# PSUM tiles for down projections, and the order and split of ready weights, in a fused attention, MoE and SwiGLU kernel

## The chip, the cores and the metric

One core of one Trainium2 chip runs the kernel. The metric is the device time of that core for one execution, in microseconds; lower is better. Before the change it is 2129.76 us, the median of three runs.

## The reference

Three stages run one after the other (setup and parameter names left out):

```python
def _attn_ref(q, k, v):
    # B, H, S, D = 4, 8, 576, 64; heads 0-3 see the last 32 positions, heads 4-7 every 32nd
    scores = scale * np.matmul(q, k.transpose(0, 1, 3, 2))
    scores = np.where(masks[None], scores, -1000000000.0)
    attn = np.exp(scores - np.max(scores, axis=-1, keepdims=True))
    return np.matmul(attn / (np.sum(attn, axis=-1, keepdims=True) + 1e-09), v)

def _moe_ref(x, w_gate, w1, w2):
    # N, D, E, F = 2304, 512, 8, 1024
    logits = x @ w_gate
    P = np.exp(logits - logits.max())
    for _ in range(8):
        P /= P.sum(1, keepdims=True) + 1e-09
        P /= P.sum(0, keepdims=True) + 1e-09
        P *= N / E
    for e in range(E):
        out += P[:, e:e + 1] * (np.maximum(x @ w1[e], 0.0) @ w2[e])
    return out

def _moe2_ref(x, w_gate, w_val, w_out, rms_g):
    # 2304 tokens, d_model 512, d_ff 1536
    xn = x / np.sqrt(np.mean(x * x, axis=-1, keepdims=True) + 1e-06) * rms_g
    g = xn @ w_gate
    return g * (1.0 / (1.0 + np.exp(-g))) * (xn @ w_val) @ w_out
```

## The kernel before

Every large matrix product is made of high and low halves in the 32-bit format fp32r, three matmuls for each product (high by high, high by low, low by high). A product of two-by-two blocks is done with seven block products in place of eight, so sums and differences of blocks ("combos") are prepared for tokens and weights, and results are added up again in several places.

The program has four stretches. Until about 320 us it runs attention and expert 0. From there to about 1600 us it runs experts 1 to 7 in 42 groups: `n` counts groups, a group is an expert `g`, a half `hh` of its width and a third `qd` of the tokens. A group has two rounds of seven up products. Each is six matmuls of 128x384 columns (L1215) into one of two PSUM tiles of a bank, `ub0` and `ub1`, which VectorE (L1247) and ScalarE (L1358, L1362) empty. After each up product stands one down unit (L1817): nine matmuls of 128x256 columns, which belong to the group 12 slots earlier. Two units make a down product `k` (0 to 6), which fills three times 256 columns of PSUM. Then `evict_1` adds these to `acc`, by ScalarE (L1838) for products 0, 2, 3 and 4 of most groups, by VectorE (L1849) for the rest, or, in the last expert, in three pieces by VectorE (L1843).

From about 1600 to 1725 us lies the transition: the last group's downs, the RMS norm, transposes of the normed tokens on TensorE (L1465, emptied at L1466 by VectorE), the splitting of them (L1482, L1483), their stores to `xnd` in HBM (L1492, L1516) and the loads of token blocks (L1147). From there to the end there are nine passes over the SwiGLU layer (a third of its width by a third of the tokens). Their up products are again L1215 (finished at L1383, L1401, L1404, L1418), and each of their downs is three matmuls of 128x512 columns (L729 to L731) into one of six PSUM banks. `evict` empties a bank by ScalarE in the first third (L2110) and by VectorE after that (L2112).

PSUM has eight banks. Two hold `ub`. The other six are a pool with three tiles, made in `begin_psum`, which follows readers and writers by the tile:

```python
pool = ctx.enter_context(tc.tile_pool(name="db", bufs=1, space=PSUM, reuse_waits="tile"))
three, two, one = (pool.tile([P, 512 * n], F32, name=f"db{n}") for n in (3, 2, 1))
threes = [three[:, :768], two[:, :768], three[:, 768:]]
```

`PAIR` gives a down product its place: products 0 and 2 write the first 768 columns of `three` (A), products 1, 3 and 5 those of `two` (B), products 4 and 6 the last 768 of `three` (C). The transposes use `one`. In the first two groups the column sums of the routing matrix (Sinkhorn) are a matmul with ones (`columns_1`, L715) into a free part of the `ub` tile just emptied; VectorE reads it at L719.

The weights of the SwiGLU layer are prepared during the experts. `first_combos` makes the combos of the first quarter's weights in high and low and stores them to `w1d` in HBM (L924), with the seven products in the order `SPOTS`; `ready_combos` loads them back during the transition (L938), one product or two at a time. Second weights lie as plain numbers in `m2o`; `prepare_2` loads one tile to a single buffer in `fa` (L1080), ScalarE writes the high half to `w2t` (L1083) and VectorE the low half (L1086).

Who runs when: each engine runs its instructions in program order. Program order comes from helper queues. `Background.pump` is called once per slot; a `Queue` gives out a step when its lag (in slots: `STEP` 1.5, `PACE` 1.2, `WRITE` 3, `READ` 7) is over, in turn; `follow` is an `add` that starts from now; `later` calls a function some slots later, outside the queues; `drain` brings a tagged step forward at the latest point of its use. Nearly all loads and stores of these stretches are issued on SyncE's queue, the `y1d` traffic on GpSimd's.

## Time and profile before

| what | value |
|---|---|
| runs | 2129.76 us median of 3 (2123.81 to 2134.14) |
| profiled execution, its own time | 2127.49 us |
| its span in the trace | 2124.7 us |
| mean granted TensorE clock | 0.985 |
| TensorE matmuls busy | 2027.7 us (95%) |
| weight loads busy (beside matmuls) | 1926.7 us (91%) |
| VectorE busy | 1594.4 us (75%) |
| ScalarE busy | 1312.5 us (62%) |
| GpSimd busy | 268.4 us (13%) |
| moved by DMA | 434.24 MB, mean 204 GB/s |

Busy shares are means over the four stretches, and TensorE's busy time contains modelled ends of matmuls, so that a short wait may not show as idle time. A weight load (PEld) stands ahead of each matmul; where it waits, the matmul behind it waits less, by what was still running. Times in the trace are counted from the span's start.

### The profile page before, as it was taken

Reading aid. Unit: us, or ns where it says so; the run is one execution under the profiler, and the core shown is the slowest. Engines: PE = TensorE matmul, PEld = TensorE weight load, DVE = VectorE, ACT = ScalarE, POOL = GpSimd, SP = SyncE. Lnnn points to the kernel's source line nnn. Section 1 sums busy time; section 2 is a strip of 40 time slices with the busy share of each in tenths; the row PEclk is TensorE's granted clock in tenths of the full one; section 3 lists DMA queues with packets and bytes.
Section 4 is the critical chain, followed back from the end, with each engine's and each line's share of the span. In section 5 each row is a group of like instructions: output and inputs, shape, how many; then the busy total and the mean of one; then the engine's idle time right before and its main releaser. Section 6 shows DMA issues by size and latency. Waiting matters only on the chain. (4 is left out here: it accounts for less than half of the span.)

```text
span 2124.7 us, 37479 instructions
## 1 busy us (share of the span) xinstructions
PE 2027.7 (95%) x13611; PEld 1926.7 (91%) x13611; DVE 1594.4 (75%) x3387; ACT 1312.5 (62%) x2932; POOL 268.4 (13%) x304
## 2 busy tenths in 40 slices
PE   8999998999999999999999999999997689999998
PEld 7888888999999999999999999999997578888897
DVE  4677656878787887868778787887987567877644
ACT  6766334777776877778777777777755333423422
POOL 6444200001111111111111111111100000000000
PEclk9999999999999999999999999999998899999999
DMA  7687675577978979798887978869657764443331
GB/s 188 165 247 197 197 250 181 210 247 178 279 210 216 264 204 296 202 245 224 237 250 193 264 185 239 225 165 281 185 158 261 232 202 155 131 174 115 129 134 60
DMA packets 358249, 434.24 MB, mean 204 GB/s; under 512 B 80944, under 2 KB 260336, under 8 KB 358064
## 3 DMA queue, kind: packets, MB, share of 16 engines
q1 hardware_dynamic: 319296, 363.48, 52.2%
q0 software_dynamic: 38768, 68.36, 18.6%
q8 instruction: 107, 1.75, 0.3%
q14 instruction: 78, 0.64, 0.1%
HBM read 301.75 MB, written 130.02 MB: 203 GB/s over the span
## 5 line engine op out<-in xcount | busy, mean ns | idle before, releaser
L1215 PE MATMUL ub<-xt,w1t 128*128 128x384 f32 x2328 | 475.4, 341 | 29.2 <-DVE fa L1404 14.2
L1215 PEld LDWEIGHTS ub<-xt,w1t 128*128 128x128 f32 x2328 | 401.5, 192 | 36.5 <-DVE fa L1404 14.8
L1215 PE MATMUL ub<-xx,w1t 128*128 128x384 f32 x1956 | 396.4, 339 | 10.5 <-DVE fa L1247 3.8
L1817 PE MATMUL db<-w2t,ht 128*128 128x256 f32 x2772 | 383.0, 283 | 6.5 <-DVE acc L1849 3.3
L1817 PEld LDWEIGHTS db<-w2t,ht 128*128 128x128 f32 x2772 | 368.2, 190 | 11.1 <-DVE acc L1849 7.1
L1817 PE MATMUL db<-w2t,hx 128*128 128x256 f32 x2520 | 349.6, 284 | 7.2 <-DVE acc L1849 3.8
L1215 PEld LDWEIGHTS ub<-xx,w1t 128*128 128x128 f32 x1956 | 333.8, 190 | 18.4 <-DVE fa L1247 6.9
L1817 PEld LDWEIGHTS db<-w2t,hx 128*128 128x128 f32 x2520 | 333.2, 190 | 16.2 <-DVE acc L1849 12.5
L1247 DVE TENSOR_TENSOR fa<-ub,fa 128x384 f32<-128x384 f32 x360 | 199.2, 554 | 149.2 <-PE ub L1215 134.9
L1366 ACT ACTIVATE fa<-fa 128x384 f32<-128x384 f32 x252 | 132.3, 525 | 180.6 <-DVE fa L1247 180.3
L1881 POOL DMA_DIRECT2D y1d<-acc x99 | 113.9, 1150 | 843.6 <-ACT acc L1874 378.3
L1243 DVE TENSOR_TENSOR ht<-fa,ht 128x384 fp32r<-128x384 f32 x344 | 189.4, 552 | 33.0 <-ACT ht L1240 32.3
L1240 ACT ACTIVATE ht<-fa 128x384 fp32r<-128x384 f32 x344 | 177.4, 518 | 37.9 <-DVE fa L1418 37.4
L1874 ACT ACTIVATE acc<-acc,prob 128x256 f32<-128x256 f32 (+1 forms) x351 | 190.8, 573 | 14.3 <-DVE acc L1849 14.0
L1243 DVE TENSOR_TENSOR hx<-fa,hx 128x384 fp32r<-128x384 f32 x316 | 174.4, 552 | 27.9 <-ACT hx L1240 26.6
L1240 ACT ACTIVATE hx<-fa 128x384 fp32r<-128x384 f32 x316 | 162.1, 519 | 48.7 <-DVE fa L1418 47.4
L1321 DVE TENSOR_TENSOR fa<-fa 128x384 f32<-128x384 f32 x336 | 185.6, 552 | 5.3 <-ACT fa L1362 0.3
L1358 ACT COPY fa<-ub 128x384 f32<-128x384 f32 x252 | 119.7, 475 | 94.9 <-PE ub L1215 90.8
L1849 DVE TENSOR_TENSOR acc<-db,acc 128x768 f32<-128x768 f32 (+1 forms) x117 | 143.0, 1222 | 33.3 <-PE db L1817 32.1
L1838 ACT COPY acc<-db 128x768 f32<-128x768 f32 x156 | 124.5, 798 | 19.8 <-PE db L1817 16.8
L1383 ACT COPY fa<-ub 128x384 f32<-128x384 f32 x108 | 51.4, 477 | 92.0 <-PE ub L1215 91.8
L981 DVE TENSOR_TENSOR w1t<-fa,w1t 128x256 fp32r<-128x256 f32 (+1 forms) x160 | 83.4, 525 | 11.1 <-ACT w1t L978 10.7
(261 smaller groups left out, 3070.2 us busy)
## 6 DMA issues: line engine op xcount, KB each, us to landing
xt<-xdt SPq DMA_DIRECT2D x111, 768.0 KB
xx<-xdt SPq DMA_DIRECT2D x92, 768.0 KB
y1d<-acc POOLq DMA_DIRECT2D x72, 384.0 KB, 7.0
y1d<-acc POOLq DMA_DIRECT2D x36, 768.0 KB, 8.1
xt<-xnd SPq DMA_DIRECT2D x25, 768.0 KB
xx<-xnd SPq DMA_DIRECT2D x24, 768.0 KB
fa<-in_moe_w_dram SPq DMA_DIRECT2D x56, 256.0 KB
raw<-in_moe_w_dram SPq DMA_DIRECT2D x52, 256.0 KB
```

The lines of the kernel that those rows point to most:

```text
L1215: nc.tensor.matmul(ps[:, :TH], w[i][:, c], x[:, k, c], start=first and c == 0 and n == 0, stop=c == 1 and n == 2, skip_group_check=True,)
L1240: nc.scalar.activation(h[0], src, func)
L1243: engine.tensor_tensor(out=h[1], in0=src, in1=h[0].bitcast(F32), op=ALU.subtract)
L1247: nc.vector.tensor_tensor(out=out, in0=ps, in1=more, op=ALU.add)
L1321: nc.vector.tensor_tensor(**kw)
L1358: nc.scalar.copy(z[nm], ps)
L1366: nc.scalar.activation(z[nm], z[nm], AF.Relu)
L1817: nc.tensor.matmul(spot(k, m), hm[x], w[y], start=BEGIN[k] and r == 0 and m in FIRST[PAIR[k]] and i == 0, stop=r == 1 and i == 2, skip_gro ...
L1838: nc.scalar.copy(a, ps)
L1849: nc.vector.tensor_tensor(out=a, in0=ps, in1=a, op=ALU.add)
L1874: nc.scalar.activation(a, a, AF.Copy, scale=prob[:, tile_of(qd, b), g : g + 1])
L1881: nc.gpsimd.dma_start(out=y, in_=t, accum_op=ALU.add)
```

## The change

It has four parts.

- PSUM: three tiles of two banks in place of tiles of three, two and one. Places A, B and C each get a tile of their own (its first 768 columns). The six bank views `db` are in the order first halves, then second halves of the three tiles; expert 0's four accumulators, the gate and the Sinkhorn head take other views.
- Transposes and column sums: transposes go by turns to the two banks of the third tile (first tile where the down product is 6), and the column sums go to a bank of that tile (of the first tile for some slots of group 1), not to `ub`.
- Ready weights: `w1d` holds products in their own order, so a store of one piece becomes two or three (80 in place of 32), and the loads get longer (14 in place of 40; the last six are written at L2079 of the new file).
- Second weights: `prepare_2` loads to the low place of `w2t` itself, soon after the call and outside the queue; ScalarE makes the high half from there, and VectorE the low half in place. The first one in the transition waits 16 slots before its high half.

```diff
@@ begin_psum
-            three, two, one = (pool.tile([P, 512 * n], F32, name=f"db{n}") for n in (3, 2, 1))
-            db = [t[:, 512 * i : 512 * (i + 1)] for t, n in ((three, 3), (two, 2), (one, 1)) for i in range(n)]
-            threes = [three[:, :768], two[:, :768], three[:, 768:]]
+            twos = [pool.tile([P, 1024], F32, name=f"db{n}") for n in range(3)]
+            db = [t[:, 512 * i : 512 * (i + 1)] for i in range(2) for t in twos]
+            threes = [t[:, :768] for t in twos]
@@ accumulators, gate, unit
-                return db[:4]
+                return [db[i] for i in (0, 1, 3, 4)]
-                place = db[4], db[5], acc[:, 0, 0], wgc2
+                place = db[2], db[5], acc[:, 0, 0], wgc2
-        FIRST = ((0, 2), (0, 2), (0, 1))
-                        spot(k, m), hm[x], w[y], start=BEGIN[k] and r == 0 and m in FIRST[PAIR[k]] and i == 0,
+                        spot(k, m), hm[x], w[y], start=BEGIN[k] and r == 0 and m != 1 and i == 0,
@@ second, the rounds
-                turn_tile(groups[m][2], t, db[5], spares[m])
+                turn_tile(groups[m][2], t, db[(2 if u < 6 else 0) + 3 * (t % 2)], spares[m])
-                        free_part = b[:, TH : TH + E]
+                        free_part = db[0 if n and 4 <= 7 * r + i < 12 else 2][:, :E]
@@ first_combos
-        def store(src, n0, n):
-            for i, t in enumerate((h[:, : src.shape[1]], src)):
-                nc.sync.dma_start(out=w1d[:, s, i, n0 : n0 + n, c], in_=t.rearrange("p (k n) -> p k n", k=n))
+        def store(src, spots):
+            for i, t in enumerate((h, src)):
+                for at, k, n in spots:
+                    nc.sync.dma_start(
+                        out=w1d[:, s, i, k : k + n, c],
+                        in_=t[:, P * at : P * (at + n)].rearrange("p (k n) -> p k n", k=n),
+                    )
-            (1, lambda: store(raw, 0, 4)), (5, lambda: high(both)), (STEP, lambda: low(both)),
-            (1, lambda: store(both, 4, 3)),
+            (1, lambda: store(raw, ((0, 0, 2), (2, 5, 1), (3, 2, 1)))), (5, lambda: high(both)), (STEP, lambda: low(both)),
+            (1, lambda: store(both, ((0, 3, 2), (2, 6, 1)))),
@@ ready_combos
-        at = region(g, j)
-        for k, n in ((), ((0, 2),), ((3, 2),), ((5, 1), (6, 1)), ((2, 1),))[part]:
-            p = SPOTS.index(k)
-            for i in range(2):
-                nc.sync.dma_start(
-                    out=at(7 * i + k, n).bitcast(F32).rearrange("p (k m) -> p k m", k=n),
-                    in_=w1d[:, j, i, p : p + n].rearrange("p k c m -> p k (c m)"),
-                )
+        k, n = ((0, 0), (0, 2), (3, 2), (5, 2), (2, 1))[part]
+        if n:
+            to = w1_flat[:, 3584 * j : 3584 * (j + 1)].rearrange("p (i k m) -> p i k m", i=2, k=7)
+            nc.sync.dma_start(
+                out=to[:, :, k : k + n].bitcast(F32), in_=w1d[:, j, :, k : k + n].rearrange("p i k c m -> p i k (c m)")
+            )
@@ prepare_2
-        t = fa[:, 4608:5120]
+        hi, t = w2t[:, i, 0], w2t[:, i, 1]
         def load():
-            conv.drain(("o", (g - E) * NG + f))
-            nc.sync.dma_start(out=t, in_=m2d["o"][:, (g - E) * NG + f, :])
+            if todo:
+                todo.clear()
+                conv.drain(("o", (g - E) * NG + f))
+                nc.sync.dma_start(out=t.bitcast(F32), in_=m2d["o"][:, (g - E) * NG + f, :])
         def high():
-            nc.scalar.activation(w2t[:, i, 0], t, AF.Copy)
+            load()
+            nc.scalar.activation(hi, t.bitcast(F32), AF.Copy)
         def low():
-            nc.vector.tensor_tensor(out=w2t[:, i, 1], in0=t, in1=w2t[:, i, 0].bitcast(F32), op=ALU.subtract)
+            nc.vector.tensor_tensor(out=t, in0=t.bitcast(F32), in1=hi.bitcast(F32), op=ALU.subtract)
-        prep2.add([(WRITE, load), (READ, high), (STEP, low)], ("w2", i))
+        bg.later(1, load)
+        prep2.follow([(wait, high), (STEP, low)], ("w2", i))
@@ evict_1
-                    prepare_2(E, (0, 2, 1, 3)[k - 3])
+                    prepare_2(E, (0, 2, 1, 3)[k - 3], LAST_READ if k == 3 else STEP)
@@ after the last group
-        for j in (2, 3):
-            for part in range(1, 5):
-                ready_combos(E, j, part)
+        for j, parts in (
+            (2, ((last_r[:, :1792], 0), (x_slot(gone_x)[:, :1280], 7), (last_r[:, 1792:], 12), (x_slot(gone_x)[:, 1280:], 13))),
+            (3, ((w2t[:, 0:3].rearrange("p f s n -> p (f s n)"), 0), (xt_flat[:, 7680:8192], 12))),
+        ):
+            ready = w1d[:, j].rearrange("p i k c m -> p (i k c m)")
+            for t, at in parts:
+                nc.sync.dma_start(out=t.bitcast(F32), in_=ready[:, 256 * at : 256 * at + t.shape[1]])
```

How this moves instructions is shown at three places. A row is the line, the operation, what it writes and reads (the number behind a name is a buffer's), its shape and which engines or DMA lanes it waits for. Lines are those of each file, so L1817 of before is L1822 of the change.

First TensorE in the expert groups, where product 0 follows product 6. Before (`db3` is the tile `three`):

```order
L1215 MATMUL ub0_4251<-xx_3899,w1t_77 128x384 [waits Activation_49]
L1215 MATMUL ub0_4251<-xx_3899,w1t_77 128x384 x5
L1817 MATMUL db3_3996<-w2t_78,hx_3900 128x256 [waits DVE_49]
L1817 MATMUL db3_3996<-w2t_78,hx_3900 128x256 x8
L1215 MATMUL ub1_4252<-xx_3899,w1t_77 128x384 x6
```

After (`db0` is the first of the three equal tiles):

```order
L1222 MATMUL ub0_4251<-xx_3899,w1t_77 128x384 [waits Activation_49]
L1222 MATMUL ub0_4251<-xx_3899,w1t_77 128x384 x5
L1822 MATMUL db0_3996<-w2t_78,hx_3900 128x256 x9
L1222 MATMUL ub1_4252<-xx_3899,w1t_77 128x384 [waits DVE_49]
L1222 MATMUL ub1_4252<-xx_3899,w1t_77 128x384 x5
```

Product 0's first matmul waited for VectorE and no longer does.

Second TensorE at the very end, the last three downs of the last pass (the same pattern stands at the end of each pass's block). Before, all three in banks of `three`:

```order
L729 MATMUL db3_3996<-w2t_78,ht_81 128x512 [waits Activation_49]
L730 MATMUL db3_3996<-w2t_78,ht_81 128x512
L731 MATMUL db3_3996<-w2t_78,ht_81 128x512
L729 MATMUL db3_3996<-w2t_78,ht_81 128x512 [waits DVE_49]
L730 MATMUL db3_3996<-w2t_78,ht_81 128x512
L731 MATMUL db3_3996<-w2t_78,ht_81 128x512
L729 MATMUL db3_3996<-w2t_78,ht_81 128x512 [waits DVE_49]
```

After, one in each tile:

```order
L730 MATMUL db0_3996<-w2t_78,ht_81 128x512 [waits DVE_49,Activation_49]
L731 MATMUL db0_3996<-w2t_78,ht_81 128x512
L732 MATMUL db0_3996<-w2t_78,ht_81 128x512
L730 MATMUL db1_3997<-w2t_78,ht_81 128x512 [waits DVE_49]
L731 MATMUL db1_3997<-w2t_78,ht_81 128x512
L732 MATMUL db1_3997<-w2t_78,ht_81 128x512
L730 MATMUL db2_3998<-w2t_78,ht_81 128x512 [waits DVE_49]
```

Before, the second and third down wait for the eviction of the down just ahead of them; after, each waits for that of the other half of its tile, three downs earlier.

Third SyncE's queue in the transition, from the last token block load (`xx`) to the first of the later stores to `xnd`. Before (36 loads from `w1d` in all):

```order
L1147 DMA xx_3899<-xnd_63 128x2x768
L1080 DMA fa_82<-m2o_69 128x512
L1492 DMA xnd_63<-acc_3898 128x6x128 [waits DMAHW6_49,Activation_49]
L1492 DMA xnd_63<-acc_3898 128x6x128 [waits DMAHW7_49,DVE_49]
L1080 DMA fa_82<-m2o_69 128x512 [waits DMAHW5_49,DMAHW0_49,DVE_49]
L938 DMA w1t_77<-w1d_66 128x256 [waits DMAHW1_49]
L938 DMA w1t_77<-w1d_66 128x256 [waits DMAHW2_49]
...
L938 DMA w2t_78<-w1d_66 128x256 [waits DMAHW4_49]
L1516 DMA xnd_63<-acc_3898 128x4x128 [waits DMAHW5_49,DMASW6_49,Activation_49]
```

After (12 loads):

```order
L1154 DMA xx_3899<-xnd_63 128x2x768
L1085 DMA w2t_78<-m2o_69 128x512 [waits PE_49]
L1085 DMA w2t_78<-m2o_69 128x512 [waits DMAHW4_49,PE_49]
L1499 DMA xnd_63<-acc_3898 128x6x128 [waits DMAHW5_49,Activation_49]
L1499 DMA xnd_63<-acc_3898 128x6x128 [waits DMAHW6_49,DVE_49]
L1085 DMA w2t_78<-m2o_69 128x512 [waits DMAHW7_49,PE_49]
L940 DMA w1t_77<-w1d_66 128x2x512 [waits DMAHW0_49]
L940 DMA w1t_77<-w1d_66 128x2x256 [waits DMAHW1_49]
...
L2079 DMA w2t_78<-w1d_66 128x3072 [waits DMAHW2_49]
L2079 DMA xt_80<-w1d_66 128x512 [waits DMAHW3_49]
L1523 DMA xnd_63<-acc_3898 128x4x128 [waits DMAHW4_49,DMASW6_49,Activation_49]
```

The load of a second weight into `fa` that waited for VectorE, ahead of the `w1d` loads, has become three loads into `w2t` that wait for TensorE, on either side of the first two `xnd` stores.

## Rows read from the trace of the kernel before

**Rows 1.** The page, part 1: span; busy us (share) xinstructions of each engine.

```profile
span 2124.7 us, 37479 instructions
PE 2027.7 (95%) x13611; PEld 1926.7 (91%) x13611; DVE 1594.4 (75%) x3387; ACT 1312.5 (62%) x2932; POOL 268.4 (13%) x304
```

**Rows 2.** Table by stretch: from:to, length, busy (xcount) by engine, PEclk, DMA share, GB/s.

```profile
400.00:1400.00 1000.00, 987.67 (x6921) 974.57 (x6921) 812.73 (x1624) 761.61 (x1583) 129.79 (x120) 1.00 0.85 231
1400.00:1500.00 100.00, 99.99 (x706) 99.04 (x705) 82.35 (x169) 73.54 (x155) 10.38 (x9) 1.00 0.75 205
```

**Rows 3.** Waits of the weight loads, 400 to 1400 us: total, times, longest.

```profile
PEld db L1817 <- DVE acc L1849: 17.1, 33, 1.7
PEld ub L1215 <- DVE fa L1247: 5.3, 6, 1.8
PEld ub L1215 <- ACT fa L1362: 2.9, 6, 0.8
```

**Rows 4.** The same of the matmuls, 320 to 1560 us.

```profile
PE db L1817 <- DVE acc L1849: 7.1, 11, 1.4
PE ub L715 <- DVE fa L1247: 4.8, 4, 2.5
```

**Rows 5.** The same of the matmuls, 1560 to 2125 us.

```profile
PE db L729 <- DVE acc L2112: 10.5, 8, 2.1
PE db L1465 <- DVE acc L1466: 3.1, 4, 1.3
PE db L729 <- ACT acc L2110: 2.3, 3, 0.9
```

**Rows 6.** Order of time, passes and tail, TensorE and VectorE: start, length, instruction, [idle before].

```profile
1987.25 0.50 PE L729 MATMUL db<-w2t,ht 128*128 128x512 f32 x1 [1.81 <-DVE acc L2112]
...
1988.25 0.69 DVE L2112 TENSOR_TENSOR acc<-db,acc 128x512 f32<-128x512 f32 x1 [1.05 <-PE db L731]
...
2117.54 0.50 PE L729 MATMUL db<-w2t,ht 128*128 128x512 f32 x1 [0.78 <-DVE acc L2112]
```

**Rows 7.** Order of time, the transition: TensorE, then ScalarE, then SyncE's queue.

```profile
1602.07 2.29 PE L1817 MATMUL db<-w2t,hx 128*128 128x256 f32 x9 [3.34 <-DVE acc L1843]
...
1637.75 4.15 PE L1215 MATMUL ub<-xt,w1t 128*128 128x384 f32 x12 [5.51 <-ACT fa L1383]
...
1660.66 2.29 PE L1215 MATMUL ub<-xt,w1t 128*128 128x384 f32 x6 [13.96 <-DVE fa L1404]
...
1632.29 0.63 ACT L1083 ACTIVATE w2t<-fa 128x512 fp32r<-128x512 f32 x1 [6.06 <-PE ub L1215]
...
1658.80 0.42 ACT L1482 ACTIVATE acc<-acc 128x256 fp32r<-128x256 f32 x1 [12.85 <-DMA xnd<-acc]
...
1618.94 1.09 SPq L1080 DMA_DIRECT2D fa<-m2o  x1
...
1633.67 0.33 SPq L1080 DMA_DIRECT2D fa<-m2o  x1
...
1654.90 1.73 SPq L1516 DMA_DIRECT2D xnd<-acc  x3
```

**Rows 8.** The instructions of L1849: ns min/median/max, first and last start, shapes.

```profile
L1849 DVE TENSOR_TENSOR acc<-db,acc x117: 947/958/1759, 358.0 to 1532.4; 128x768 f32<-128x768 f32 x78, 128x1536 f32<-128x1536 f32 x39
```

**Rows 9.** Order of time on TensorE, a column sum and what follows.

```profile
341.43 0.60 PE L715 MATMUL ub<-cv,ones 128*128 128x8 f32 x2 [2.46 <-DVE fa L1247]
341.88 4.19 PE L1215 MATMUL ub<-xx,w1t 128*128 128x384 f32 x12
```

**Rows 10.** The stores of ready weights, L924, on SyncE: ns min/median/max.

```profile
L924 SPq DMA_DIRECT2D w1d<-cv x32: 359/360/462, 923.0 to 1187.8; - x32
```

**Rows 11.** Table by stretch, columns as in rows 2.

```profile
1618.00:1634.00 16.00, 13.79 (x96) 13.14 (x95) 11.55 (x23) 2.76 (x7) 0.00 (x0) 0.90 0.98 368
1634.00:1656.00 22.00, 8.95 (x40) 8.47 (x40) 8.34 (x21) 9.93 (x25) 1.70 (x2) 0.75 0.87 284
1920.00:2000.00 80.00, 74.74 (x385) 68.01 (x385) 56.99 (x121) 30.77 (x68) 0.00 (x0) 1.00 0.19 63
```

More of the change, by code (lines that the diff above doesn't have):

```diff
@@ L172 @@
     READ = 7
+    LAST_READ = 16
     STEP = 1.5
@@ L881, in conversion @@
                 conv.add([(step, whole), (WRITE, store)], tag)
-    SPOTS = (0, 1, 5, 2, 3, 4, 6)
     def first_combos(s, c):
@@ L1059, in prepare_1 @@
         if g == E:
-            prep.add([(PACE, lambda: ready_combos(g, j, part))], ("w1", g, j))
+            prep.add([(PACE, lambda: ready_combos(j, part))], ("w1", g, j))
         else:
@@ L1769 @@
                 sink = Queue(bg)
-                sink.add([(1.5, f) for f in steps] + sinkhorn_head(cv[:, :256], db[4:]))
+                sink.add([(1.5, f) for f in steps] + sinkhorn_head(cv[:, :256], (db[2], db[5])))
                 sink.add([(2, lambda: rows(totals))], "head")
```

5 lines of the change are left out of this document (3 added, 2 removed).

## The prediction

> **What bounds the kernel now.** I read the page's first part before anything else: TensorE's matmuls are busy for 2027.7 of 2124.7 us, VectorE for three quarters of that span and ScalarE for less [rows 1]. So this is a TensorE kernel with some 97 us of matmul idle time, and a change that adds no matmul and takes none away can only move that idle time, and the time at half clock that follows it. The next view is the table by stretch. In the middle, from 400 to 1400 us, TensorE is idle for 12.3 us in 1000; a stretch without gaps holds 706 matmuls in 100 us, and this one holds 6921 in 1000, so by the count it loses (7060 - 6921) / 7.06 = 19.7 us [rows 2]. The count finds more than the idle time because the modelled end of a matmul covers short waits. The chip grants 1.00 of the 2.4 GHz there.
>
> Then the table of waits, for that part of the program: weight loads of the down units (L1817) wait 33 times for VectorE's eviction at L1849, 17.1 us in all [rows 3], of which some 7 us show as gaps at the matmul itself; the column sums (L715) wait 4.8 us for the eviction of `ub` [rows 4]. In the last 565 us TensorE waits 10.5 us for L2112 and 2.3 us for L2110, the evictions of the second FFN [rows 5]. The order of time says where: in the nine passes, in gaps like the one of 1.81 us, and in three of 0.78 us in the tail [rows 6]; the transition from experts to passes has the two largest gaps of this part, 5.51 us for L1383 and 13.96 us for L1404 [rows 7].
>
> **1. Three PSUM tiles of two banks.** In the order of before, product 0's first down matmul stands behind VectorE's eviction of product 6, although the two write different banks for the most part: both are views of the tile `three`. Only one `ub` product of about 1.05 us stands between them, and the eviction alone takes 0.96 us at 768 columns and 1.76 us at 1536 [rows 8]. In the new order this wait is gone, as is product 4's wait for product 2; product 2 behind 0 and product 6 behind 4 stay. Bounds: 7.1 us, the gaps seen at the matmul [rows 4], and 17.1 us, all that the weight loads waited [rows 3]. The count lies between: in 400 to 1400 us 19.7 us are lost, against 17.1 + 5.3 + 2.9 = 25.3 us of weight-load waits, so 0.78 of such a wait is real and 17.1 x 0.78 = 13.3 us. Some of it comes back: TensorE arrives earlier at the `ub` evictions L1247 and L1362, which already cost 8.2 us of weight-load time there. I take **-12 us**, between gap and count and nearer the count. In the last group the same wait is L1843's 3.34 us gap [rows 7]; VectorE works without a pause there, so half of it: **-1.5 us** (0 to 3.3).
>
> **2. The passes.** The downs of a block go to three pairs of halves. Before, a down into the second bank of `two` waits for the eviction of its first bank, just written: 10.5 us for L2112 and 2.3 us for L2110 [rows 5]. In the new order a tile's other half is reached three downs later, and a down lasts about 0.70 us (three matmuls 0.23 us apart), so an eviction of 0.69 us [rows 6] has some 1.4 us of other downs over it. The tail's three gaps (2.3 us) are not all gained, since the evictions then run back to back at 0.69 us each, just the pace of the downs. Bounds 8 (10.5 without the tail's 2.3) and 12.8; I take **-10 us**.
>
> Here a rule of the Trainium skill bears. What the rows show: in the passes a down into one bank waits for an eviction of another bank [rows 6], so the wait follows the tile, not the bank. The Trainium skill's page "PSUM — Partial Sum Buffer", section "PSUM bank collisions raise a hardware error", asks for a guard by bank and 32-partition quadrant, as two engines in one of these at once end in an error and not in a stall; by it the passes' wait between banks of one tile is not needed at all. The trace disagrees only in that the program guards more widely than this; if the wait followed the bank, the sum would lose this part and come to about 10 us more.
>
> **3. Column sums and transposes in the idle pair.** The column sums (eight in the first two groups) leave the free part of `ub`, so L715 no longer waits for an eviction of `ub` and the next product no longer waits for L719: 4.8 us seen at the matmul of L715 [rows 4]. After the longest of these gaps, 2.46 us, the next two products take 4.19 us where two take some 2.1: the half clock, 1.2 GHz, for about 2 us more [rows 9]. Bounds 0 (VectorE is itself late there, and the sums' own inputs come from it) and 9 (all four gaps, each with its stretch at half clock: 4.8 + 2.1 and as much again for the shorter three); I take **-3 us**. The transposes now alternate between two halves of the idle tile: their waits for L1466 are 3.1 us [rows 5], mostly in the transition and counted there.
>
> **4. Weights in order of use, and the split in place.** The stores of the ready weights become 80 DMAs in place of 32, between 923 and 1188 us. At 0.36 to 0.46 us of issue each 48 more cost SyncE at most 22 us of 265 [rows 10]; nothing on TensorE waits for SyncE there, so **0**; what it costs without that cover is the slow rival below. The loads are where the gain could be. Before, ScalarE stands at L1083 for 6.06 us; the row names a product of TensorE, but what was late, I take it, is the load of the one buffer, issued at 1618.94 behind seven block loads (5.5 MB, some 15 us at the 368 GB/s of that stretch). SyncE's second `fa<-m2o` is issued only at 1633.67, behind VectorE's low half, and holds the w1d loads until 1634.06; 36 loads later, at 1654.90, come the `xnd` stores of the next tokens, and ScalarE (12.85 us) waits for one of them to land before it may overwrite `acc`; TensorE waits 13.96 us on the chain behind it [rows 7]. After, the loads go straight to `w2t`, the first high half stands some 16 ticks later, and 12 loads in place of 36 stand between. But the transfers also limit: the block loads up to 1634 run at a DMA share of 0.98 and 368 GB/s, and the w1d loads at 0.87 and 284 GB/s [rows 11]. Their 6.29 MB (a table is 7 products x 2 halves x 256 numbers of 4 bytes x 128 partitions = 1.84 MB; two products of each of the first two tables are loaded earlier) take 22 us at 284 GB/s and 17.1 us at 368. If longer pieces bring 340 GB/s, 18.5 us, they end at about 1652.5 in place of 1656, and with a shorter queue the store lands some 4.5 us sooner. Add 2 us for the transposes' waits. Bounds: 0 (bandwidth sets all) and 19.5 (5.51 + 13.96 gone). I take **-7 us**, nearer the transfer bound, as its rows are full.
>
> The second weights' in-place loads in the passes wait for TensorE's last read of their place and block SyncE for that time; the DMA share is 0.19 there [rows 11], and the loads behind it have room, so 0. Small new waits: the gate and Sinkhorn head now share tile `db2`, and transposes at u = 6 wait for product 2's eviction: **+1 us** (0 to 5).
>
> **Sum.** -12 - 1.5 - 10 - 3 - 7 + 1 = -32.5 us. The profiled execution took 2127.5 us (a span of 2124.7 and 2.8 around it): 2095.0. It lies 2.3 us under the median of the three runs, 2129.8, from which the same sum gives 2097.3; I forecast **2096 us**. With the bounds: least 7.1 + 8 - 5 = 10 us, most 17.1 + 3.3 + 12.8 + 9 + 19.5 = 62 us.
>
> **The rivals.**
> (a) *VectorE takes over.* The waits removed are waits for VectorE. If the bubbles only move to the next `ub` eviction, part 1 gives its 7.1 us and the passes 8: 2127.5 - 15 = 2112. For it: VectorE is busy for 81% of that part, and L1247 already ends waits [rows 2, 3]. Against: in 1400 to 1500 us it has the same load and TensorE is busy for 99.99 [rows 2]. Chance 0.10.
> (b) *The waits follow banks.* Then the passes keep their 10 us and part 1 gives most of its 12, as product 0 shares only its last third with product 6: 2106. That the order shows the waits gone speaks against it. Chance 0.05. The Trainium skill's page named in part 2 states the rule behind this case.
> (c) *The transition gives all.* If the SyncE queue and ScalarE's block, not bandwidth, set the 13.96 us, it and its half-clock stretch go: 12.5 us more, about 2084. For it: ScalarE and VectorE have nothing to do from 1645 to 1659. Chance 0.15.
> (d) *The transition gives nothing*, the change doing there only what bandwidth undoes: 2103. For it: the DMA share of 0.87 to 0.98 [rows 11]. Chance 0.15.
> (e) *Slower: the 48 extra stores hold back x blocks.* In the order of the instructions SyncE's DMAs take turns on eight lanes, so one waits for the one eight before it. With six more in each of eight sets, about two more block landings of 3.3 us (768 KB at 231 GB/s [rows 2]) may be waited for per set, 8 x 6.6 = 53 us of SyncE. It decides once TensorE gets its x block more than 32.5 / 8 = 4.1 us late per set; at the full 6.6 us, 2127.5 - 32.5 + 53 = 2148. Against: no wait of TensorE on a DMA stands among the waits of that part, where the smallest listed is 2.9 us [rows 3], so the blocks arrive with room to spare. Chance 0.05.
>
> **How the numbers follow.** My forecast has 0.50 and the rivals 0.10, 0.05, 0.15, 0.15 and 0.05. From 2078 to 2117 lie the forecast with most of its bounds, (a), (b), (c) and (d); (e) and the far ends are left out, under 2 in 10. A measurement tells 0.5%, 10.6 us, from no change: faster means under 2119. The forecast, (b), (c) and (d) lie there, with most of (a): 0.90. The rest of (a), and a forecast near its least gain, are the same: 0.07. Slower, most of (e): 0.03.
>
> **What would show it.** Right: from 400 to 1400 us over 6990 matmuls, and the row L1817 <- L1849 nearly gone; no L729 <- L2112 row above 2 us; no gap before L715; the w1d loads issued before 1632 with the last `xnd` landing near 1654 on before's scale; the gap before L1215 at L1404 under 10 us. Wrong: the same count of matmuls with larger rows for L1247 or L1362 (a), waits in the passes as before (b), new rows of L1215 behind DMAs between 923 and 1188 us (e).

## The result, and the profile after

The changed kernel takes 2096.77 us (median of four runs, 2093.68 to 2099.58) against 2130.44 us for the kernel before. The ratio is 0.9845 with a 95% interval of 0.9815 to 0.9875, so it is faster by 33.7 us. The forecast was 2096. Its profiled execution took 2093.68 us, with a span of 2091.9 us, 32.8 us less than before. The page, part 1, stands against [rows 1]:

```profile
span 2091.9 us, 37504 instructions
...
PE 2009.6 (96%) x13611; PEld 1920.0 (92%) x13611; DVE 1591.9 (76%) x3387; ACT 1305.5 (62%) x2932; POOL 268.1 (13%) x304
```

TensorE's matmul idle time fell from 97.0 to 82.3 us; the other 18.1 us of the gain are busy time that went, for the same 13611 matmuls. The mean granted clock was 0.985 in the profiled execution before and 0.993 in this one; how much of the busy time was half clock and how much modelled ends of stalled matmuls is not separated over the whole span.

The table by stretch of the changed kernel answers to [rows 2, 11]; its columns are those of rows 2:

```profile
400.00:1400.00 1000.00, 986.38 (x6932) 981.64 (x6932) 812.32 (x1629) 755.44 (x1580) 128.85 (x119) 1.00 0.85 231
1618.00:1634.00 16.00, 12.74 (x80) 11.73 (x79) 13.43 (x31) 11.06 (x28) 1.70 (x2) 1.00 1.07 389
1634.00:1656.00 22.00, 10.61 (x61) 10.00 (x60) 10.09 (x20) 7.45 (x17) 0.00 (x0) 0.77 0.92 308
```

From 400 to 1400 us, 6932 matmuls stand where 6921 stood: almost nothing was gained in the groups of this execution. The waits say where it went. The weight loads from 400 to 1400 us, against [rows 3]:

```profile
PEld ub L1222 <- DVE fa L1254: 14.9, 12, 5.2
```

and the matmuls from 320 to 1560 us, against [rows 4]:

```profile
PE ub L1222 <- DVE fa L1254: 13.8, 11, 5.0
PE db L716 <- DVE cv L713: 1.5, 1, 1.5
```

L1849's 17.1 us (its line is L1854 now) are gone without a rest, and so are the column sums' 4.8 us, of which 1.5 us came back in another wait. But the wait for L1247 (now L1254), VectorE's eviction of `ub`, grew from 5.3 to 14.9 us at the weight loads. At the matmul it had been 3.9 us before:

```profile
PE ub L1215 <- DVE fa L1247: 3.9, 5, 1.6
```

The last stretch, 1560 us to the end, against [rows 5]:

```profile
PE ub L1222 <- DVE fa L1411: 15.3, 6, 11.4
PE ub L1222 <- DVE fa L1254: 13.8, 11, 3.9
```

The waits for L2112 and L2110 in the passes are gone. In the order of time the transition now reads as follows, TensorE, ScalarE and SyncE's queue, against [rows 7]:

```profile
1626.06 2.38 PE L1222 MATMUL ub<-xt,w1t 128*128 128x384 f32 x12 [2.20 <-ACT fa L1390]
...
1646.05 2.29 PE L1222 MATMUL ub<-xt,w1t 128*128 128x384 f32 x6 [11.39 <-DVE fa L1411]
...
1644.18 0.42 ACT L1489 ACTIVATE acc<-acc 128x256 fp32r<-128x256 f32 x1 [10.78 <-DMA xnd<-acc]
...
1621.94 3.93 SPq L940 DMA_DIRECT2D w1t<-w1d  x6
...
1633.16 7.17 SPq L1523 DMA_DIRECT2D xnd<-acc  x3
```

The 5.51 us gap is 2.20 us, the 13.96 us gap is 11.39 us. The loads of ready weights begin at 1621.94 in place of 1634.06, the later token stores at 1633.16 in place of 1654.90.

Where the time went is best read from points that mark equal work: the first and the last start of the evictions at L1849, and the first start of the passes' evictions at L2110. The instructions of the first, after, against [rows 8]:

```profile
L1854 DVE TENSOR_TENSOR acc<-db,acc x117: 949/959/1758, 354.0 to 1524.5; 128x768 f32<-128x768 f32 x78, 128x1536 f32<-128x1536 f32 x39
```

Those of L2110 before, and of the same line (L2119) after; the columns are shortest, median and longest ns, first and last start:

```profile
L2110 ACT COPY acc<-db x18: 566/586/602, 1724.1 to 1836.9; 128x512 f32<-128x512 f32 x18
```

```profile
L2119 ACT COPY acc<-db x18: 566/582/592, 1707.3 to 1817.8; 128x512 f32<-128x512 f32 x18
```

| stage | before us | after us | gain | forecast |
|---|---|---|---|---|
| start to first L1849 (the first column sums are at its end) | 358.0 | 354.0 | 4.0 | 3 |
| first to last L1849 (groups) | 1174.4 | 1170.5 | 3.9 | 12 |
| last L1849 to first L2110 (last group, transition) | 191.7 | 182.8 | 8.9 | 7 + 1.5 |
| first L2110 to the end (passes) | 400.6 | 384.6 | 16.0 | 10 |

The forecast took off 1 us more for small new waits. The sum came out within a microsecond, and two of its four stages did not: 8 us too much for the groups stand against 6 us too little for the passes. These are single executions, and a stage varies: the first one, 354.0 us here, took 356.2 and 359.5 us in after_again and old_second, which have the same program there. The last column sums, up to 384.1 us before and 377.4 us after, lie in the second stage, and 2.7 of its 3.9 us were gained ahead of the last of them.

### The profile page after: what moved, and what is told of

Same layout as the page of the kernel before. It is cut to its first block, busy times and chain, and to the rows that moved or that the text cites. A ratio compares the mean times of both kernels' runs of the same rounds, so it can differ in the third digit from the quotient of the medians.

```text
span 2091.9 us, 37504 instructions
## 1 busy us (share of the span) xinstructions
PE 2009.6 (96%) x13611; PEld 1920.0 (92%) x13611; DVE 1591.9 (76%) x3387; ACT 1305.5 (62%) x2932; POOL 268.1 (13%) x304
## 5 line engine op out<-in xcount | busy, mean ns | idle before, releaser
L1222 PE MATMUL ub<-xt,w1t 128*128 128x384 f32 x2328 | 471.5, 339 | 34.3 <-DVE fa L1254 17.8
L1222 PEld LDWEIGHTS ub<-xt,w1t 128*128 128x128 f32 x2328 | 396.5, 190 | 43.3 <-DVE fa L1254 21.6
L1222 PE MATMUL ub<-xx,w1t 128*128 128x384 f32 x1956 | 394.4, 338 | 10.2 <-DVE fa L1254 5.2
L1822 PE MATMUL db<-w2t,ht 128*128 128x256 f32 x2772 | 382.2, 282 | 3.0 <-DVE ht L1250 1.6
L1822 PEld LDWEIGHTS db<-w2t,ht 128*128 128x128 f32 x2772 | 369.5, 190 | 3.8 <-DVE ht L1250 1.9
L1822 PE MATMUL db<-w2t,hx 128*128 128x256 f32 x2520 | 347.2, 282 | 3.4 <-ACT hx L1247 2.0
L1222 PEld LDWEIGHTS ub<-xx,w1t 128*128 128x128 f32 x1956 | 331.0, 189 | 19.6 <-DVE fa L1254 8.4
L1822 PEld LDWEIGHTS db<-w2t,hx 128*128 128x128 f32 x2520 | 334.4, 189 | 4.8 <-ACT hx L1247 2.5
L1254 DVE TENSOR_TENSOR fa<-ub,fa 128x384 f32<-128x384 f32 x360 | 199.2, 554 | 129.9 <-PE ub L1222 122.4
L1250 DVE TENSOR_TENSOR ht<-fa,ht 128x384 fp32r<-128x384 f32 x344 | 189.6, 552 | 29.3 <-ACT ht L1247 28.7
L1879 ACT ACTIVATE acc<-acc,prob 128x256 f32<-128x256 f32 (+1 forms) x351 | 190.7, 572 | 15.2 <-DVE acc L1854 14.3
L1247 ACT ACTIVATE ht<-fa 128x384 fp32r<-128x384 f32 x344 | 177.3, 518 | 32.8 <-DVE fa L1425 32.3
L1250 DVE TENSOR_TENSOR hx<-fa,hx 128x384 fp32r<-128x384 f32 x316 | 174.6, 552 | 29.0 <-ACT hx L1247 27.8
L1247 ACT ACTIVATE hx<-fa 128x384 fp32r<-128x384 f32 x316 | 162.2, 519 | 48.0 <-DVE fa L1425 44.5
L1854 DVE TENSOR_TENSOR acc<-db,acc 128x768 f32<-128x768 f32 (+1 forms) x117 | 143.0, 1222 | 31.8 <-PE db L1822 31.1
```

Of the source, the lines that this page charges most:

```text
L1222: nc.tensor.matmul(ps[:, :TH], w[i][:, c], x[:, k, c], start=first and c == 0 and n == 0, stop=c == 1 and n == 2, skip_group_check=True,)
L1247: nc.scalar.activation(h[0], src, func)
L1250: engine.tensor_tensor(out=h[1], in0=src, in1=h[0].bitcast(F32), op=ALU.subtract)
L1254: nc.vector.tensor_tensor(out=out, in0=ps, in1=more, op=ALU.add)
L1822: nc.tensor.matmul(spot(k, m), hm[x], w[y], start=BEGIN[k] and r == 0 and m != 1 and i == 0, stop=r == 1 and i == 2, skip_group_check=True,)
L1854: nc.vector.tensor_tensor(out=a, in0=ps, in1=a, op=ALU.add)
```

## The experiments

Each is compared with the kernel before on the same chip (2128.6 to 2130.1 us there); differences to the changed kernel (2096.77 us, taken beside 2130.44) go across chips. Stage times are taken as in the table above, each from one execution.

### The two halves, and the stores

First question: what ate the gain in the groups? The gap rows of the changed kernel, TensorE and then VectorE:

```profile
665.96 2.01 PE L1222 MATMUL ub<-xt,w1t 128*128 128x384 f32 x6 [3.50 <-DVE fa L1254]
...
943.18 2.29 PE L1222 MATMUL ub<-xt,w1t 128*128 128x384 f32 x6 [5.02 <-DVE fa L1254]
...
665.14 0.30 DVE L838 TENSOR_SCALAR cv<-cv 128x256 f32<-128x256 f32 x1 [3.74 <-DMA m2g<-cv]
...
942.04 0.62 DVE L900 TENSOR_TENSOR cv<-cv 128x128 f32<-128x128 f32 x2 [8.32 <-DMA cv<-m2g]
```

TensorE waits for VectorE's eviction of `ub` for 3.50 and 5.02 us, and VectorE stands idle ahead of it, held by a DMA: at L838, a step of the conversion of SwiGLU weights, by a store (`m2g<-cv`), and at L900, a step of the combos, by a load (`cv<-m2g`). The second lies among the 80 stores, so the first theory was that these hold back SyncE.

**psum_parts**: the kernel before with the edits of `begin_psum`, `accumulators`, the places of the gate and the Sinkhorn head, `unit`, `turn_tile`'s bank and `free_part`, and no other.

> The kernel before with the PSUM half of the change alone: three tiles of two banks, transposes and column sums in the idle pair; weights stored, loaded and split as before. Theory (the split stores delay SyncE and with it VectorE's combos, which ate half of the gain in the groups): without them the groups gain about 9 us in place of 4, column sums 4, passes 16, transposes and last group 2: about 31 us less than before, 2099 us, and no wait over 2 us of L1215's successor for VectorE near 943 us. Rival (VectorE's own load caps the groups at some 4 us whatever the stores): about 26 us less, 2104 us, with the 5 us wait still there.

Measured: 2103.52 us, ratio 0.9874 (0.9844 to 0.9905), 26 us less than before. Groups 1162.6 us (11.8 less), transition 188.2 (3.5 less), passes 390.7 (9.9 less). The wait near 943 us was 1.94 us, but one of 3.34 us stood near 664 us, where no ready weights are stored. The median is the rival's, the stage the theory's, but the profiled execution (2097.39 us) ran 6 us under the median; neither is settled by it.

**weights_only**: the changed kernel with those edits undone.

> The changed kernel with the old PSUM tiles, transposes and column sums, so that only the weights half is left (80 stores, 14 loads, second weights split in place). Theory: transition 7 to 9 us less, from 3 to 5 us given back in the groups by the stores: about 4 us less than before, 2126 us. Rival 1 (the stores cost nothing): 8 us less, 2122 us. Rival 2 (the transition is bound by bandwidth, and what the changed kernel gained there came from PSUM): 0 to 5 us more than before.

Measured: 2125.75 us, ratio 0.9984 (0.9965 to 1.0002): 3.6 us less than before and, at the edge of its interval, no difference. Transition 185.3 us, 6.4 less than before; passes 399.9, as before; groups 1187.3, which is 12.9 us more than before. Both halves together give 25.8 + 3.6 = 29.4 us of the 33.7.

The profiled execution was one of the slowest of twelve (2131.51 us), and its groups show why. With the old tiles TensorE waits as long for the `ub` eviction as in the changed kernel:

```profile
PEld ub L1222 <- DVE fa L1254: 14.8, 5, 6.2
```

```profile
583.12 1.31 PE L1222 MATMUL ub<-xt,w1t 128*128 128x384 f32 x6 [2.73 <-DVE fa L1254]
...
677.22 2.29 PE L1222 MATMUL ub<-xt,w1t 128*128 128x384 f32 x6 [4.91 <-DVE fa L1254]
```

Up to the first store of ready weights near 923 us this program does what the kernel before does, and the trace of before has no gap of even 0.9 us near these two places. A third gap, near 957 us, is 5.98 us long.

**few_stores**: 32 stores as before, and the first pass looks up products where they lie.

```diff
+    SPOTS = (0, 1, 5, 2, 3, 4, 6)
-            (1, lambda: store(raw, ((0, 0, 2), (2, 5, 1), (3, 2, 1)))), (5, lambda: high(both)), (STEP, lambda: low(both)),
-            (1, lambda: store(both, ((0, 3, 2), (2, 6, 1)))),
+            (1, lambda: store(raw, ((0, 0, 4),))), (5, lambda: high(both)), (STEP, lambda: low(both)),
+            (1, lambda: store(both, ((0, 4, 3),))),
-        k, n = ((0, 0), (0, 2), (3, 2), (5, 2), (2, 1))[part]
+        k, n = ((0, 0), (0, 2), (4, 2), (6, 1), (2, 2))[part]
-                        product((a, b)[which], w_block(region(E + p, s), wk), x_view(xmap[xk]), begins)
+                        product((a, b)[which], w_block(region(E + p, s), wk if p else SPOTS.index(wk)), x_view(xmap[xk]), begins)
```

> The changed kernel with the ready weights stored in the old order, 32 stores in place of 80, and loaded with as few loads as in the change, because the first pass looks its products up in the stored order. Theory (split stores cost some 5 us near 943 us): 3 to 5 us less than the changed kernel, 2092 to 2094 us, and the wait of 5.0 us at the `ub` product there falls under 2 us. Rival (VectorE's load or the transfers themselves are late there, not SyncE's order): within 1.5 us of the changed kernel, with the wait still there.

Measured: 2097.18 us, ratio 0.9842 (0.9817 to 0.9868), the changed kernel's time. The same place on TensorE:

```profile
943.11 2.29 PE L1224 MATMUL ub<-xt,w1t 128*128 128x384 f32 x6 [2.26 <-DVE fa L1256]
```

The gap is shorter in this execution, but not gone, and the median did not move: the theory of the stores falls. Forecast and result agree on this term (0). The Trainium skill's page "DMA: Bandwidth & Descriptors", section "Rules for kernel authors", advises to coalesce many small transfers into large ones. Here 80 stores or 32 made no difference; in the changed kernel TensorE waits for no DMA from 320 to 1560 us.

**tiles_only**: the kernel before with the tiles alone. The transposes stay in `db[5]`, which is now the bank that products 4 and 6 also sum in, so some of these sums are overwritten; only its time is read.

> The kernel before with only the three equal PSUM tiles; transposes stay in one bank (now one half of the third tile), column sums stay in `ub`. Theory: all but the column sums' 4 us and the transposes' 2 us of what the PSUM half gives: about 25 us less than before, 2105 us; waits for L1849 in the down units and for L2112 in the passes gone. Rival (the transposes' bank now shares a tile with products 4 and 6, so they wait for each other): 20 us less or under, with new waits at the transposes.

Measured: 2111.47 us, ratio 0.9907 (0.9877 to 0.9937), 17.9 us less: under the theory's 25 and within the rival's 20 or less. The rival's new wait is there, at the products that share the transposes' tile:

```profile
PE db L1817 <- DVE acc L1466: 4.0, 3, 1.7
```

Passes 389.8 us, 10.8 less than before, with no row of L729 behind an eviction. In the groups only 1.4 us were gained, and the reason stands in the order of time on TensorE:

```profile
675.57 2.29 PE L1215 MATMUL ub<-xt,w1t 128*128 128x384 f32 x6 [4.82 <-DVE fa L1247]
...
953.37 2.29 PE L1215 MATMUL ub<-xt,w1t 128*128 128x384 f32 x6 [5.68 <-DVE fa L1247]
```

About as long as in the changed kernel or longer, at the same places, in a kernel with 32 stores. With weights_only, which has them with the old tiles, the gaps belong neither to the stores nor to the tiles. Against weights_only, whose gaps are about as long, the groups here take 14.3 us less.

### The gaps that took the gain

**after_again**: the changed kernel, unaltered.

> The changed kernel once more, unaltered, for a second profile. The theory that the split stores are late is out, since 32 stores gave the same time. New theory: in every third group (the last of an expert half, where weights are prepared) VectorE stands at a conversion step whose DMA lands late, and how late differs from execution to execution; so the three largest gaps (1.31, 3.50 and 5.02 us near 573, 666 and 943 us) come at the same places with other lengths, at least one of them over 1 us longer or shorter. Rival (their length is set by the program): the same lengths within 0.3 us.

Its time was 2100.33 us. The three gaps:

```profile
576.63 1.95 PE L1222 MATMUL ub<-xt,w1t 128*128 128x384 f32 x6 [2.26 <-DVE fa L1254]
...
672.26 2.29 PE L1222 MATMUL ub<-xt,w1t 128*128 128x384 f32 x6 [5.58 <-DVE fa L1254]
...
948.05 2.29 PE L1222 MATMUL ub<-xt,w1t 128*128 128x384 f32 x6 [5.14 <-DVE fa L1254]
```

2.26, 5.58 and 5.14 us where the first profile had 1.31, 3.50 and 5.02. The places are set by the program, the lengths by the execution. By the count of up products (84 matmuls of L1222 to a group) they lie in groups 8, 11 and 20, each the last of an expert half. After the two longer ones the next six matmuls take 2.29 us in place of 1.31, at a granted clock of 0.50.

**pause_last**: conversions rest in the last group of an expert half, not in the first.

```diff
-            conv.paused = n % NQD == 0 and n < NGP - 3
+            conv.paused = n % NQD == NQD - 1 and n < NGP - 9
```

> The changed kernel with the conversions of SwiGLU weights paused in the last group of each expert half in place of the first, so that no conversion step stands in VectorE's order where those gaps are. Theory (VectorE is held by a late DMA of the conversion): the gaps over 1 us near 573, 666 and 943 us go, 6 to 10 us less than the changed kernel, 2087 to 2091 us. Rival (VectorE's or ScalarE's own load in those groups holds the `ub` evictions): gaps stay or move to the groups after, within 2 us of the changed kernel.

Measured: 2103.95 us, ratio 0.9883 (0.9859 to 0.9906): 7 us slower than the changed kernel, with intervals that just overlap; the groups take 1180.3 us. The gaps at the old places went, but the waits of the matmuls from 320 to 1560 us became:

```profile
PE ub L1222 <- DVE fa L1254: 10.5, 13, 2.0
PE db L1822 <- DVE hx L1250: 5.0, 9, 0.8
PE db L1822 <- DVE ht L1250: 3.2, 2, 2.7
```

The conversions stood in other groups and held VectorE there, now ahead of the low halves (L1250) that the downs need as well. Moving the steps does not help; the miss speaks for the DMA and against those groups' load, but does not decide it.

**late_heads**: three slots more between load and first step. So that all conversions still end in time, they no longer rest after group 20.

```diff
-    CONV_WAIT = (6, 4)
-    PRE_WAIT = 6
+    CONV_WAIT = (9, 4)
+    PRE_WAIT = 9
-            conv.paused = n % NQD == 0 and n < NGP - 3
+            conv.paused = n % NQD == 0 and n < NGP - 21
```

> The changed kernel with the first step of each conversion and of each combo 9 slots after its load in place of 6 (some 6 us more for the DMA), and the conversions no longer paused after group 20 so that they still end in time. Theory: the waits of VectorE for conversion loads fall from 8 us to about 2, those for the stores stay partly: 3 to 8 us less than the changed kernel. Rival (own load): no change within 2 us, or slower, as the conversions now stand elsewhere.

Measured: 2079.86 us, ratio 0.9778 (0.9755 to 0.9802), 17 us less than the changed kernel, twice the most that was expected. The stretch from 400 to 1400 us, and the matmuls' wait for the `ub` eviction from 320 to 1560 us:

```profile
400.00:1400.00 1000.00, 998.59 (x7052) 995.20 (x7051) 830.07 (x1661) 768.81 (x1607) 130.48 (x121) 1.00 0.85 234
```

```profile
PE ub L1222 <- DVE fa L1254: 1.3, 4, 0.7
```

VectorE's own waits for these DMAs from 320 to 1560 us, all rows added up, are 25.6 us in the kernel before, 38.7 us in the changed one and 3.0 us here, most of it in one row:

```profile
DVE cv L900 <- DMA cv<-m2v: 2.4, 1, 2.4
```

7052 matmuls in 1000 us are nearly the 706 per 100 of a stretch without gaps, and VectorE does its work at 83% busy. So VectorE's own load costs TensorE next to nothing here; it was held by DMAs that landed after its turn. The run has two edits, but the three gaps lie before group 21, where the conversions rest as before, so it is the later first step that removed them. The groups take 1152.3 us.

**late_before**: the same three lines in the kernel before.

> The kernel before with the late first steps of conversions and combos alone. Theory (two things bound the groups in turn: product 0's wait for the shared tile, and VectorE held by late conversion DMAs; with one removed the other takes its place): 6 to 9 us less than before, 2120 to 2123 us, and the wait rows for L1849 keep their 17 us at the weight loads. The difference of this run to late_heads in the groups is then what the tiles are worth without that cover, 12 to 15 us as predicted. Rival (late heads are simply worth 17 us in any kernel): 2112 us.

Measured: 2117.72 us, ratio 0.9951 (0.9934 to 0.9969), 11.7 us less than before, between theory (6 to 9) and rival (17). The weight loads' waits, against [rows 3]:

```profile
PEld db L1817 <- DVE acc L1849: 14.1, 33, 1.0
PEld ub L1215 <- ACT fa L1362: 1.0, 5, 0.4
PEld ub L1215 <- DVE fa L1247: 0.9, 1, 0.9
```

The wait for the shared tile is still there, the one for `ub` nearly gone. The groups take 1165.5 us. Against late_heads that is 13.2 us, of which 2.3 us lie ahead of the last column sum: some 11 to 13 us are what the tiles are worth in the groups when VectorE is on time. The forecast had 13.3 us by the count, and took 12.

### Column sums, second weights, transition

**old_columns**: one line back.

```diff
-                        free_part = db[0 if n and 4 <= 7 * r + i < 12 else 2][:, :E]
+                        free_part = b[:, TH : TH + E]
```

> The changed kernel with the column sums back in the free part of `ub`. By the prediction's term 3 us more than the changed kernel (0 to 9), 2100 us, with four gaps before L716 of 4.8 us in sum and the half-clock stretch near 340 us back. Rival (VectorE is late there in any case, the gap only changes its name): within 1 us.

Measured: 2098.66 us (2096.53 to 2109.39), ratio 0.9873 (0.9848 to 0.9899): 2 us above the changed kernel, with intervals that overlap. The stage is clearer. From the first to the last column sum 57.0 us pass here, 52.3 us in the changed kernel (L716 starts at 325.1 and 377.4 there): 4.7 us. And the gap is back:

```profile
PE ub L716 <- DVE fa L1254: 4.8, 4, 2.5
```

**old_second**: `prepare_2` and its call as before.

> The changed kernel with second weights loaded to one buffer and split from there as before. Theory: ScalarE is blocked for some 6 us again and holds SyncE's loads of ready weights, so the transition takes 3 to 5 us more: 2100 to 2102 us, groups and passes as in the changed kernel. Rival (the transition is set by the bytes ahead of the token stores, not by the order): within 1 us.

Measured: 2097.96 us, ratio 0.9866 (0.984 to 0.9891): the medians don't tell it from the changed kernel. Its profiled execution was the slowest of six, so its stages are to be read with care: transition 187.9 us against 182.8 and, in after_again, 183.9; passes 389.8 against 384.6 in both. On TensorE:

```profile
1635.37 3.83 PE L1216 MATMUL ub<-xt,w1t 128*128 128x384 f32 x12 [5.45 <-ACT fa L1384]
...
1655.56 2.29 PE L1216 MATMUL ub<-xt,w1t 128*128 128x384 f32 x6 [11.57 <-DVE fa L1405]
```

The 5.45 us gap at the first product is that of before [rows 7], so the block of ScalarE is what the in-place split removed; the large gap stays as long as after. About 4 us in the transition are shown in one trace, not in the medians.

In the passes the difference is mostly one of clock. Their stretch in before, after, old_second and psum_parts, columns as in rows 2:

```profile
1724.10:2124.70 400.60, 374.50 (x1887) 337.59 (x1887) 271.62 (x613) 135.04 (x282) 0.00 (x0) 0.99 0.37 127
1707.30:2091.90 384.60, 369.08 (x1887) 334.82 (x1887) 270.73 (x613) 134.63 (x282) 0.00 (x0) 1.00 0.39 132
1718.50:2108.30 389.80, 373.35 (x1888) 338.48 (x1886) 269.84 (x609) 134.35 (x282) 0.00 (x0) 0.98 0.38 130
1704.80:2095.50 390.70, 374.12 (x1888) 338.72 (x1887) 271.15 (x614) 134.56 (x282) 0.00 (x0) 0.98 0.38 130
```

old_second and psum_parts, with the new tiles and the old split, leave TensorE idle for about as long as the changed kernel (16.5 and 16.6 us against 15.5), but their matmuls are busy for 4 to 5 us more at a lower mean clock: after a gap of 2.72 us twelve matmuls took 3.69 us in old_second, after the same gap, 2.34 us long, 2.71 us in the changed kernel. Added up over stretches of 4 us, what the clock lacked of full speed in the passes is worth 6.0 us before, 6.1 and 6.2 us in these two, and nothing in the changed kernel.

**late_ready**: on top of late_heads, the last six loads of ready weights go behind token stores.

```diff
-            ready = w1d[:, j].rearrange("p i k c m -> p (i k c m)")
-            for t, at in parts:
-                nc.sync.dma_start(out=t.bitcast(F32), in_=ready[:, 256 * at : 256 * at + t.shape[1]])
+            def whole(j=j, parts=parts):
+                ready = w1d[:, j].rearrange("p i k c m -> p (i k c m)")
+                for t, at in parts:
+                    nc.sync.dma_start(out=t.bitcast(F32), in_=ready[:, 256 * at : 256 * at + t.shape[1]])
+            prep.add([(READ, whole)], ("w1", E, j))
```

> late_heads with the last six loads of ready weights (3.67 MB, used from the third round of the first pass on) put in the weights' queue, so that five token stores go ahead of them. Theory (the large gap of the transition is the wait for a token store that lands behind those bytes; 3.67 MB at 308 to 390 GB/s are 9 to 12 us): the gap of 12 us at the `ub` product falls under 6 us and the time by 5 to 9 us against late_heads, 2071 to 2075 us. Rival (the bytes must pass in any case, and TensorE waits for them a little later): the same time within 2 us, with new waits for `last_r` or `w2t`.

Measured: 2075.82 us, ratio 0.9752 (0.9733 to 0.977), 4 us less than late_heads, with intervals that overlap a little. The matmuls' waits from 1595 to 1665 us:

```profile
PE ub L1222 <- DMA w2t<-w1d: 4.0, 1, 4.0
PE ub L1222 <- DMA last_r<-w1d: 3.9, 1, 3.9
...
PE ub L1222 <- DVE fa L1411: 2.0, 1, 2.0
PE ub L1222 <- DMA xt<-w1d: 1.0, 1, 1.0
```

The gap had been this one in late_heads:

```profile
1627.37 2.29 PE L1222 MATMUL ub<-xt,w1t 128*128 128x384 f32 x6 [11.99 <-DVE fa L1411]
```

It is 2.0 us now, as the theory says, and 8.9 us of waits for the late weights take its place, as the rival says: they went too far back.

**soon_ready**: the same loads 4 and 10 slots late.

```diff
-            prep.add([(READ, whole)], ("w1", E, j))
+            bg.later(4 if j == 2 else 10, whole)
```

> late_ready with its six loads 4 and 10 slots after their old place, so that five to seven token stores go ahead of the first four and five more ahead of the last two, in place of twelve and more. In late_ready the gap of 12 us fell to 2, and 9 us of new waits for `last_r`, `xt` and `w2t` came in its place. Theory (order decides: both can be in time): new waits under 4 us and the store's wait under 4 us, 2069 to 2073 us. Rival (the bytes of this stretch decide, order only moves the wait): sum of the gaps from 1600 to 1660 us as in late_ready, 2074 to 2078 us.

Measured: 2068.5 us (2064.69 to 2072.58), ratio 0.971 (0.9692 to 0.9727): 28 us less than the changed kernel, 11 us less than late_heads, and the fastest of all. In the same stretch no wait for ready weights is left, and the two largest rows are

```profile
PE ub L1222 <- DVE fa L1254: 3.6, 3, 2.0
PE ub L1222 <- DVE fa L1411: 3.3, 2, 2.4
```

The transition takes 174.2 us against 184.2 in late_heads and 182.8 in the changed kernel. The bytes are those of late_heads; only the order of SyncE's queue changed.

## Why the prediction was right, and where it was wrong

**The total and the sign** were right: 2096.77 us against 2096, and faster beyond doubt. The terms were not all right: two errors of 6 to 8 us cancelled, and that the total came within a microsecond is luck. By the prediction's own signs, two that it named for being right did not come: over 6990 matmuls from 400 to 1400 us (6932), and under 10 us for the gap at L1404 (11.39). A third came in part: a gap of 1.5 us is left before the column sums.

**Part 1, tiles in the groups (-12 us): right in its working, 8 us too large for the profiled executions.** The groups gained 3.9 us, and by the second profile 0.8, while the wait for L1247 went from 3.9 to 13.8 us at the matmul. The step that did not hold there is "Some of it comes back: TensorE arrives earlier at the `ub` evictions L1247 and L1362": the forecast let 1.3 us of 13.3 come back, and put down to TensorE's early arrival what hangs on late DMAs. Most of the growth is not the tiles' doing, since weights_only has 14.3 us of this wait with the old tiles: VectorE's steps of the conversions and combos waited for DMAs, and in the one execution profiled before the change these waits were short. With VectorE on time the tiles are worth 11 to 13 us (late_before against late_heads). By the medians the whole change is worth 37 us with late heads in both kernels (each against before on its chip) and 33.7 us without, so some 3 us is what these waits took from it, a difference within the intervals. Rival (a) named the place but not the cause. The trace of before showed the wait too, on VectorE just ahead of TensorE's gap:

```profile
946.32 0.62 DVE L901 TENSOR_TENSOR cv<-cv 128x128 f32<-128x128 f32 x2 [4.91 <-DMA cv<-m2g]
```

```profile
947.47 1.31 PE L1215 MATMUL ub<-xt,w1t 128*128 128x384 f32 x6 [1.61 <-DVE fa L1247]
```

I read TensorE's waits and not what VectorE waited for behind them.

**The last group and the transition (-1.5 and -7 us): right in size**, 8.9 us; so rival (d) is out. psum_parts shows 3.5 of it and weights_only 6.4. But "nearer the transfer bound, as its rows are full" took the remaining 11.39 us for bandwidth. It was order: the token store waited for 3.67 MB that nobody needed yet, and soon_ready gained 10.0 us on late_heads in that stage without a byte less. Rival (c) was nearer the truth of the kernel than the forecast; the change just didn't collect it.

**Part 2, the passes (-10 us): right for the waits, too small for the whole change, 16.0 us.** The rows for L2112 and L2110 went, the tail's three gaps with them; that the evictions would set the tail's pace did not show. TensorE's idle time in the passes fell by 10.6 us (26.1 to 15.5), as forecast. The other 5.4 us are busy time of the same matmuls, most of it the half clock behind the gaps, a term that the forecast left out here though its part 3 counts it. The tiles without the in-place split do not collect it all (389.8 and 390.7 us in old_second and psum_parts, at a mean clock of 0.98), the change does (384.6 us in both its traces, at 1.00), and weights_only, without the tiles, gained only 0.7 us. Why the gaps that are left are a little shorter with the in-place split, no single wait shows, and old_second's median does not show the gain; this stays open.

**Part 3, column sums (-3 us): right within its bounds**, 4.7 us by old_columns' trace.

**Part 4, the stores (0): right**, by few_stores. Rival (e), late x blocks by 48 more stores, had no place.

**Rival (b)**, waits by bank: out. After the change no down of the passes waits for an eviction, though the same banks are written and read. The Trainium skill's page "PSUM — Partial Sum Buffer", section "PSUM bank collisions raise a hardware error", asks for a guard by bank and quadrant; by that rule the trace agrees that the waits between banks of one tile were the program's own. No run here puts two engines in one bank at a time.

## What to carry to other kernels

A wait that is removed is worth its row only if the engine behind it is on time: look one link further, at what the releasing engine itself waits for, before taking the sum. VectorE ran its steps in program order, so one that waited for a DMA delayed the evictions behind it (8.32 us at L900), and three slots more between issue and use were worth as much as the tiles alone (17 us here, 18 us in tiles_only). Where a large gap ends with a store or a load, ask first which bytes are ahead of it in its queue and when they are needed. The Trainium skill's page "DMA: Bandwidth & Descriptors", section "Rules for kernel authors", says to issue early and wait late; late_heads agrees, with three slots more between the two, some 6 us by an estimate from 28 us for a group of 14 slots (42 groups in 1174 us).

## What was not expected of the hardware

Executions of one kernel differ by about 6 us (2093.68 to 2099.58 for the changed kernel) to 17 us (2118.18 to 2135.48 in weights_only), and three gaps near 573, 666 and 943 us, set by when a conversion's DMA lands, account for some of it: 9.8 us of gaps in one execution of the changed kernel, 13.0 in the other, without the half clock behind them. A gap costs more than itself once TensorE comes out of it at the lower of its two levels: after 1.31 us of idle time six matmuls took 1.33 us at a granted clock of 1.00, after 5.02 us they took 2.29 us at 0.50. The first of the two:

```profile
572.78 1.33 PE L1222 MATMUL ub<-xt,w1t 128*128 128x384 f32 x6 [1.31 <-DVE fa L1254]
```
